# Last-tile bias by a one-row product, sums off GpSimd, and a new instruction order in a fused attention and dense kernel

## The chip, the cores and the metric

The kernel runs on one core of one Trainium2 chip. The metric is the device time of one launch in microseconds. Before the change the median of three runs is 163.94 us (163.46 to 164.64). The profiled execution took 163.67 us; the span of its trace, from the first instruction to the last, is 162.0 us.

A core has four engines that compute side by side: TensorE (PE, matrix products into PSUM), VectorE (DVE), ScalarE (ACT, activations) and GpSimd (POOL). SyncE (SP) starts most of the transfers (DMA). Each engine works through its own list of instructions in order, and engines wait for each other by semaphores. PSUM has 8 banks, each with 512 fp32 columns on 128 partitions.

## What is computed

The input is 2048 tokens of 448 bf16 values. After a layer norm, a windowed attention (16 heads, each token sees itself and seven earlier ones at a distance of two) and a two-layer dense branch with gelu run on the same normed tokens. The dense branch, through silu, gates the attention branch:

```python
def _B_ref(x, w1, b1, w2, b2):
    h = jnp.einsum("bsd,df->bsf", x, w1) + b1
    h = _gelu(h)
    return jnp.einsum("bsf,fd->bsd", h, w2) + b2

x = A_x
xn = _layernorm(x, axis=-1)
s = _A_ref(xn, A_wqkv, A_wo)      # attention, then its output product with wo
g = _silu(_B_ref(xn, B_w1, B_b1, B_w2, B_b2))
return x + s * g
```

silu(y) is computed as 0.5 * y * (tanh(y / 2) + 1), so that ScalarE needs only tanh. The inner width of the dense branch is 1792, that is 14 blocks of 128.

## The kernel before

Tokens are worked on in 16 tiles of 128 and in 4 chunks of 4 tiles. The kernel is not written in the order in which it runs. It is first written as a list of tasks with an engine, an estimated cost, dependencies, buffers and a priority; a planner goes through them in estimated time, and where several tasks could start on an engine it takes the one with the highest priority. The order that comes out is emitted, and is fixed on the chip. A task may name two engines; the planner then takes the one on which it ends first.

The first dense layer (FF1) of a chunk makes 14 blocks of h. Its contraction is 448 = 3 x 128 + 64, so each block takes three full products (`full`) and one on 64 rows (`tail`). Two tails on different halves of the array run side by side. A batch closes some blocks (full products, then the tail) and opens others (tail, then full products), so that its tails lie together:

```python
FF1 = (((3, 3), (2, 2), (2, 2)),      # per chunk: (closed, opened) of each batch
       ((3, 5), (3, 3)),
       ((2, 3), (2, 3), (2, 2)),
       ((4, 4), (2, 4)))
JOINED = (False, False, False, True)
```

```python
def batch(close, opened, prio):
    for j in close:
        ...  # three full products of j, taking a PSUM bank: L572 for FF1
    pairs = max(sum(j.half == h for j in every) for h in range(2))
    ...      # all tails of the batch, in pairs on the two halves: L575 for FF1
    for i, j in enumerate(opened):
        ...  # three full products of j
```

Each block leaves PSUM by a gelu on ScalarE (L579). Queries, keys and values are made in the same way (L513, L539 full; L516, L542 tails; `if JOINED[c] or not c` puts the values of a chunk into the batches of its queries and keys). The attention has products on 32 rows (QK, L651), an exp on ScalarE (L657), a mask on VectorE (L665) and the product with the values (L673).

The second dense layer of a tile, and what follows it up to the gate:

```python
def parts(t):
    n = D // 2 if t == NT - 1 else D          # the last tile goes in two halves of 224 columns
    return [(slice(c0, c0 + n), n, c0 + n == D) for c0 in range(0, D, n)]

def ff2_part(t, cs, n, end, prio):
    ...
        for mt in range(7 * i, 7 * i + 7):                               # L608, twice seven
            nc.tensor.matmul(ps[:, :n], h[...][:, j * P:(j + 1) * P], w2[:, mt, cs],
                             start=(mt == 0), stop=(mt == NMT - 1))
    ...
    def f2(k):                                                           # L624, y
        nc.vector.tensor_tensor(out=y[:, :n], in0=bank[:, :n], in1=b2[:, cs], op=ALU.add)
    def f3(k):                                                           # L630, tanh
        nc.scalar.activation(t[:, :n], y[:, :n], ACT.Tanh, scale=0.5)
    def f4(k):                                                           # L634, gate
        nc.vector.scalar_tensor_tensor(out=g[:, :n], in0=t[:, :n], scalar=1.0,
                                       in1=y[:, :n], op0=ALU.add, op1=ALU.mult)
```

(Buffer look-ups are shortened to the names of the tiles here.) The end of a tile starts when its attention is there and its dense part is done:

```python
def final_part(t, cs, n, g, prio):
    def f1(k):                                # L715: the output product, four matmuls
        ...
    a = plan.add("PE", pe(n, KT), f1, [t_oT[t]] + t_wo + [t_f2[t]], ...)
    def f2(k):                                # L720: sg = 0.5 * bank * g
        ...
    def f3(k):                                # L725: o = x + sg
        (nc.gpsimd if k.on == "POOL" else nc.vector).tensor_tensor(...)
    last = NT - 3 <= t < NT - 1
    o = plan.add(("DVE", "POOL") if last else "DVE", (dve(n, 2), 1.3) if last else dve(n, 2), f3, [s], ...)
    ...                                       # L732: the store, issued by SyncE
```

For tile 15 `t_f2` is the second half, so both of its output products come after all of its dense products. The gates of the last tiles lie in the buffer of `w_in`, which is free by then, and appear under that name in the trace.

Of the kernel before, what the change touches and what calls it, by code (L numbers as in the profile page):

```python
# [10 lines left out]
ALU = mybir.AluOpType  # L11
ACT = mybir.ActivationFunctionType
# [141 lines left out]
def kernel(  # L154
# [12 lines left out]
    nc = tc.nc  # L167
    P = 128
    S, D, H, DH, F = A_x.shape[1], 448, 16, 28, 1792
    assert tuple(A_x.shape) == (1, S, D) and S == 2048  # L170
    NT = S // P
# [4 lines left out]
    NMT = F // P  # L176
# [24 lines left out]
    def sb(name, shape, dt=BF16):  # L201
        return const.tile(shape, dt, name=name)
# [3 lines left out]
    x_sb = sb("x_sb", [P, NT, D])  # L206
# [8 lines left out]
    b2 = sb("b2", [P, D])  # L215
# [5 lines left out]
    ident = sb("ident", [P, P])  # L221
    eps_t = sb("eps_t", [P, 1], F32)
    half_t = sb("half_t", [P, 4], F32)
    m_gen = sb("m_gen", [P, 4, NQ])
    m_b0 = sb("m_b0", [P, 4, P])
    m_sp = sb("m_sp", [P, 4, NQ])
# [5 lines left out]
    def ring(name, n, shape, dt=BF16, fifo=False):  # L232
# [8 lines left out]
    p_y = ring("y", 2, [P, D], F32)  # L241
    p_t = ring("t", 2, [P, D], F32)
    p_g = ring("g", 4, [P, D])
    p_sg = ring("sg", 2, [P, D])
    p_o = ring("o", 3, [P, D])
# [6 lines left out]
    p_b = _Pool([psum.tile([P, 512], F32, name=f"bank{i}") for i in range(8)])  # L252
# [2 lines left out]


    FF1 = (((3, 3), (2, 2), (2, 2)),
           ((3, 5), (3, 3)),
           ((2, 3), (2, 3), (2, 2)),
           ((4, 4), (2, 4)))  # L260
    JOINED = (False, False, False, True)

    PRIO = {
                "project": (1, 122.5, 82, 27.5,),
                "project2": (164, 164.5, 166, 26.5,),
                "values": (186.5, 199, 146, 47,),
                "attn": (199, 199, 199, 167.5, 153.5, 147, 112.5, 99, 190, 169, 144, 105, 100, 84.5, 82,
            41.5, 31,),
                "ff1": (117, 79, 37, 125.5, 114.5, 15.5, 195, 187, 127.5, 198.5, 157, 4.5,),
                "gelu": (48, 103, 17, 103,),  # L270
                "ff2": (50, 55, 82, 88, 187.5, 82, 34, 14.5, 58.5, 5.5, 53.5, 9, 23.5, 102.5, 13.5, 1,),
                "final": (31.5, 36.5, 21.5, 191, 80.5, 62, 10.5, 20, 5.5, 67.5, 5.5, 1, 35.5, 37.5, 1, 1,),
                "norm": (173, 139.5, 108.5, 30, 30.5, 69.5, 156, 89.5, 71.5, 197, 51, 46, 85, 195, 51.5,
            70.5,),
                "stats": (59, 70, 70.5, 136.5, 65.5, 151.5, 60.5, 122.5, 172, 169, 93.5, 69, 64, 184.5,
            38.5, 57.5,),
                "turn_x": (92, 52, 134, 5, 66, 175, 52.5, 61.5, 30, 199, 125, 104.5, 32.5, 198, 196, 199,),
                "turn_qk": (89, 93, 5, 26, 185.5, 169, 35, 199, 51, 140, 126.5, 33.5, 18, 171, 118, 119.5,),
                "turn_o": (115, 170, 118, 26.5, 59, 153, 1, 8.5, 32, 37.5, 131, 1, 197, 192.5, 29.5,
            153.5,),  # L280
                "move_v": (52.5, 67.5, 27.5, 24.5, 1, 9.5, 90, 60, 161, 134.5, 168, 24, 192, 190.5, 1, 178,
            68.5,),
                "move_o": (106.5, 32, 154, 199, 148, 97, 97.5, 109.5, 57, 4.5, 76, 102.5, 178, 102.5, 28.5,
            103.5, 192.5,),
                "copies": (70, 169.5, 47.5, 44, 112, 161.5, 198.5, 181, 140.5, 16, 74, 140.5, 116, 199,
            81.5,),
    }
    LATER = {"qk": -30, "v": -27.5, "gelu": -30, "exp": 27.5, "mask": -29, "pv": -26, "recip": 9, "os": 26, "y": 60, "tanh": 49, "g": 49, "sg": 59, "o": 5.5}

    plan = _Plan()  # L290

    def buf(pool, owner, i=0):
        return pool.bufs[owner.slots[pool][i]]

    def pe(n, k=1):
        return k * (n / 2400.0 + 0.0025)

    def act(n):
        return 0.15 + n / 1130.0

    def dve(n, r=1):
        return 0.15 + n / (960.0 * r)
# [8 lines left out]
    def memset(eng, ap, v):  # L311
        def fn(_):
            getattr(nc, eng).memset(ap, v)
        return fn

    warm = p_h.bufs[-1]
    t_on = plan.add("DMA", 0.8, lambda _: None, (), 100)
# [15 lines left out]
    t_qz = [plan.add("DVE", 0.08, memset("vector", q[:, :, :, DH:], 0.0), [t_on], prio=95) for q in qk_tok]  # L333
    t_vw = [plan.add("DVE", 0.08, memset("vector", v[:, :, DH:], 1.0), [t_on], prio=96) for v in v_tok[:9]]
    t_os = [plan.add("POOL", 0.1, memset("gpsimd", o[:, D:], 0.0), [t_on], prio=94) for o in p_ot.bufs]
    t_wo = [plan.add("POOL", 0.45, memset("gpsimd", wo[64:, 3, :], 0.0), [t_on], prio=93)]
    t_E = [plan.add("POOL", 0.1, memset("gpsimd", e[:, :, NQ:], 0.0), [t_on], prio=95) for e in p_E.bufs]

# [225 lines left out]
    t_h = {}  # L564
# [22 lines left out]
    t_g = {}  # L587
    t_f2 = {}
    ff1_last = {}
# [10 lines left out]

    def ff2_part(t, cs, n, end, prio):
        c, j = divmod(t, TPC)
        halves = []
        for i in range(2):
            def f1(k, i=i):
                ps = buf(p_b, halves[0] if i else k)
                for mt in range(7 * i, 7 * i + 7):
                    nc.tensor.matmul(ps[:, :n], buf(*h_at[(c, mt)])[:, j * P:(j + 1) * P], w2[:, mt, cs],  # L608
                                     start=(mt == 0), stop=(mt == NMT - 1))
            if i:  # L610
                last = j == TPC - 1 and end
                halves.append(plan.add(
                    "PE", pe(n, 7), f1, [halves[0]] + [t_h[(c, mt)] for mt in range(7, NMT)] + t_w2[1]
                    + ([t_f2[q] for q in range(c * TPC, t)] if last else []),
                    prio + 0.5, give=tuple(h_at[(c, mt)] for mt in range(NMT)) if last else (),
                    tail=0.15))
            else:
                halves.append(plan.add("PE", pe(n, 7), f1, [t_h[(c, mt)] for mt in range(7)] + t_w2[0] + [ff1_last[c]],
                                       prio, take=(p_b,)))
        a = halves[1]  # L620
        t_f2[t] = a

        def f2(k):
            nc.vector.tensor_tensor(out=buf(p_y, k)[:, :n], in0=buf(p_b, halves[0])[:, :n], in1=b2[:, cs], op=ALU.add)  # L624
        if t == NT - 1:
            prio += 9
        y = plan.add("DVE", dve(n), f2, [a, t_b2], prio + LATER["y"], take=(p_y,), give=((p_b, halves[0], 0),))

        def f3(k):
            nc.scalar.activation(buf(p_t, k)[:, :n], buf(p_y, y)[:, :n], ACT.Tanh, scale=0.5)  # L630
        th = plan.add("ACT", act(n), f3, [y], prio + LATER["tanh"], take=(p_t,), table=("exp", "gelu"))

        def f4(k):
            nc.vector.scalar_tensor_tensor(out=buf(p_g, k)[:, :n], in0=buf(p_t, th)[:, :n], scalar=1.0,  # L634
                                           in1=buf(p_y, y)[:, :n], op0=ALU.add, op1=ALU.mult)
        t_g[t].append(plan.add("DVE", dve(n), f4, [th, y], prio + LATER["g"], take=(p_g,), give=((p_y, y, 0), (p_t, th, 0))))


    t_oT, ot_at = {}, {}
# [71 lines left out]
    def final_part(t, cs, n, g, prio):  # L711
        def f1(k):
            ps = buf(p_b, k)
            for kt in range(KT):
                nc.tensor.matmul(ps[:, :n], oT[:, kt, t * P:(t + 1) * P], wo[:, kt, cs],  # L715
                                 start=(kt == 0), stop=(kt == KT - 1))
        a = plan.add("PE", pe(n, KT), f1, [t_oT[t]] + t_wo + [t_f2[t]], prio, take=(p_b,), tail=0.15)

        def f2(k):
            nc.vector.scalar_tensor_tensor(out=buf(p_sg, k)[:, :n], in0=buf(p_b, a)[:, :n], scalar=0.5,  # L720
                                           in1=buf(p_g, g)[:, :n], op0=ALU.mult, op1=ALU.mult)
        s = plan.add("DVE", dve(n), f2, [a, g], prio + LATER["sg"], take=(p_sg,), give=((p_b, a, 0), (p_g, g, 0)))

        def f3(k):
            (nc.gpsimd if k.on == "POOL" else nc.vector).tensor_tensor(  # L725
                out=buf(p_o, k)[:, :n], in0=x_sb[:, t, cs], in1=buf(p_sg, s)[:, :n], op=ALU.add)
        last = NT - 3 <= t < NT - 1
        o = plan.add(("DVE", "POOL") if last else "DVE", (dve(n, 2), 1.3) if last else dve(n, 2), f3, [s], prio + LATER["o"],
                     take=(p_o,), give=((p_sg, s, 0),))

        def f4(_):
            nc.sync.dma_start(rows(o_half, t * P, P)[:, cs], buf(p_o, o)[:, :n])  # L732
        q = plan.add("SP", 0.55, f4, [o], 50)
        plan.add("DMA", 0.4, lambda _: None, [q], 50, give=((p_o, o, 0),), tail=1.2)
# [48 lines left out]
    def project(c):  # L783
# [19 lines left out]
        for b in blocks_of[c]:  # L803
# [11 lines left out]
    t_w2 = [[dma("POOL", w2[:, 7 * i:7 * i + 7, :], B_w2[F // 2 * i:F // 2 * (i + 1), :].rearrange("(m p) c -> p m c", p=P),  # L815
                 784, 84 - i, [t_hold])] for i in range(2)]
# [9 lines left out]
    for c, what in ((0, "F"), (1, "F"), (0, "A"), (1, "A"), (2, "F"), (2, "A"), (3, "A"), (3, "F")):  # L826
# [5 lines left out]
        else:  # L832
# [4 lines left out]
            i = 0  # L837
# [46 lines left out]
```

The softmax here doesn't subtract the row's maximum and nothing guards it: scores larger than these inputs give would overflow.

## Time and profile before

| | busy, us | share of the span | instructions |
|---|---|---|---|
| VectorE | 102.6 | 63% | 275 |
| ScalarE | 102.0 | 63% | 186 |
| GpSimd | 48.3 | 30% | 106 |
| DMA, 16 engines | | moved 20.80 MB, 128 GB/s | |

The granted TensorE clock is 0.987 of full speed. Line numbers such as L608 are those of the kernel before; in the changed kernel they move by some lines. The profile has a page (shares, the span in 40 slices, the chain of work that ended last, the costliest groups) and views on request, such as the instructions in order of time. In such a view a line gives the start in us, the duration in us, the engine, the line, the operation, what is written and read, the shapes, and at the end, in brackets, how long the engine sat idle before it and what released it. An "x7" means seven instructions merged into one line. In the chain, each piece is counted from the end of the one before it, so that its durations add up to the span, while durations of single matmuls overlap.

### The profile page before, as it was taken

The page shows a single profiled execution, that of the slowest core. Times are in us where ns is not written, and L with a number is a line of the kernel's source. Part 1 is how long each engine was busy: PE and PEld are TensorE (multiplying, and loading weights), DVE is VectorE, ACT ScalarE, POOL GpSimd, SP SyncE. Part 2 cuts the span into 40 slices and gives each one's busy share as a digit, 9 for nine tenths or more (in the row PEclk, how much of TensorE's full clock was granted, in tenths as well). Part 3 has the DMA queues.
Part 4 walks back from the last instruction along what each step waited for, and adds up shares of the span by engine and source line. Part 5 has one row for each costly group of instructions (what it writes and reads, how often), then busy time and mean ns, then how long its engine had stood idle before and what let it go on. Part 6 is the DMA issues. An engine that isn't in the chain of part 4 may idle for free.

```text
span 162.0 us, 3570 instructions
## 1 busy us (share of the span) xinstructions
PE 153.2 (95%) x1303; PEld 75.7 (47%) x1311; DVE 102.6 (63%) x275; ACT 102.0 (63%) x186; POOL 48.3 (30%) x106
## 2 busy tenths in 40 slices
PE   6999999999999999999999999999999999999940
PEld 2554333434444555445553334555555535455730
DVE  4978530395523988589892524897899994506760
ACT  3326597557587727788849577888798596722200
POOL 7306601971700050445735000037333300300020
PEclk9999999999999999999999999999999999999995
DMA  5999893799998252773968410067932450330110
GB/s 153 325 302 278 169 202 65 231 369 199 99 193 163 58 119 59 124 107 96 170 133 201 96 41 28 28 62 161 199 84 59 108 131 28 109 70 0 59 45 12
DMA packets 40733, 20.80 MB, mean 128 GB/s; under 512 B 34160, under 2 KB 38724, under 8 KB 40716
## 3 DMA queue, kind: packets, MB, share of 16 engines
q1 hardware_dynamic: 37372, 13.61, 44.0%
q0 software_dynamic: 3200, 6.85, 16.3%
q8 instruction: 10, 0.16, 0.5%
q10 hardware_dynamic: 144, 0.11, 0.3%
q14 instruction: 7, 0.06, 0.1%
HBM read 7.06 MB, written 1.84 MB: 55 GB/s over the span
## 4 chain that ended last, share of the span: by engine, by line
PE 90%; DVE 3%; issue 2%; DMA 2%; ACT 0%; DVEq 0%; ACTq 0%
PE bank L608 25%; PE bank L572 23%; PE bank L513 12%; PE bank L715 7%; PE bank L539 6%; PE bank L673 5%; PE bank L575 5%; PE bank L651 3%; PE bank L516 2%; DMA x_sb<-in_A_x_dram 2%; PE bank L542 1%; PE bank L443 1%; DVE st L397 1%; DVE y L624 1%; DVE sg L720 0%
## 5 line engine op out<-in xcount | busy, mean ns | idle before, releaser
L608 PE MATMUL bank<-w,h 128*128 128x448 bf16 (+1 forms) x238 | 46.6, 341 | 0.0
L579 ACT ACTIVATE h<-bank,b 128x512 bf16<-128x512 f32 x56 | 34.1, 696 | 9.9 <-PE bank L575 8.3
L572 PE MATMUL bank<-xnT,w 128*128 128x512 bf16 x160 | 38.0, 379 | 0.7 <-issue 0.5
L657 ACT ACTIVATE E<-bank 128x480 bf16<-128x480 f32 (+1 forms) x68 | 33.4, 580 | 6.6 <-PE bank L651 5.5
L348 POOL DMA_DIRECT2D ot<-os x31 | 16.7, 541 | 52.9 <-DVE os L685 50.1
L608 PEld LDWEIGHTS <-h 128*128 128x128 bf16 x238 | 21.9, 97 | 17.3 <-issue 0.2
L572 PEld LDWEIGHTS <-w 128*128 128x128 bf16 x168 | 15.7, 98 | 21.1 <-issue 3.8
L348 POOL DMA_DIRECT2D v<-v_tok x30 | 16.3, 548 | 29.8 <-PE bank L673 12.3
L665 DVE TENSOR_TENSOR E<-E,m_gen 128x480 bf16<-128x480 bf16 x60 | 21.4, 400 | 2.6 <-ACT E L657 2.3
L513 PE MATMUL bank<-w_in,xnT 128*128 128x448 bf16 x96 | 22.1, 352 | 0.0
L630 ACT ACTIVATE t<-y 128x448 f32<-128x448 f32 (+1 forms) x17 | 9.5, 559 | 16.0 <-DVE y L624 15.7
L624 DVE TENSOR_TENSOR y<-bank,b 128x448 f32<-128x448 f32 (+1 forms) x17 | 10.1, 594 | 7.5 <-PE bank L608 7.3
L715 PE MATMUL bank<-wo,oT 128*128 128x448 bf16 (+1 forms) x68 | 14.4, 341 | 0.0
L306 ACT CAST qk_tok<-bank 128x448 bf16<-128x448 f32 x22 | 11.3, 540 | 4.3 <-PE bank L513 2.2
L673 PEld LDWEIGHTS <-E 128*128 128x128 bf16 x272 | 10.6, 96 | 6.3 <-DVE g L634 0.7
L720 DVE SCALAR_TENSOR_TENSOR sg<-bank,g 128x448 bf16<-128x448 f32 x10 | 6.2, 620 | 9.9 <-ACT h L579 9.5
L539 PE MATMUL bank<-w_in,xnT 128*128 128x448 bf16 x48 | 11.9, 353 | 0.0
L513 PEld LDWEIGHTS <-xnT 128*128 128x128 bf16 x96 | 8.2, 97 | 7.3 <-issue 1.1
L431 DVE TENSOR_SCALAR xn<-x_sb,mv,rstd 128x448 bf16<-128x448 bf16 x16 | 6.4, 397 | 8.1 <-POOL rstd L418 4.5
L673 PE MATMUL bank<-v,E 128*128 128x29 bf16 x240 | 11.1, 176 | 0.0
L306 ACT CAST v_tok<-bank 128x448 bf16<-128x448 f32 x11 | 5.8, 536 | 8.3 <-PE bank L542 4.7
L685 DVE TENSOR_TENSOR os<-bank,rd 120x448 bf16<-120x448 f32 (+1 forms) x17 | 10.6, 624 | 0.6
(66 smaller groups left out, 135.5 us busy)
## 6 DMA issues: line engine op xcount, KB each, us to landing
out_dram<-o SPq DMA_DIRECT2D x15, 112.0 KB, 1.7
w<-in_B_w_dram POOLq DMA_DIRECT2D x2, 784.0 KB, 7.6
w<-in_B_w_dram SPq DMA_DIRECT2D x2, 672.0 KB, 6.9
w_in<-in_A_wqkv_dram SPq DMA_DIRECT2D x3, 336.0 KB, 4.4
x_sb<-in_A_x_dram POOLq DMA_DIRECT2D x2, 448.0 KB, 4.2
w<-in_B_w_dram SPq DMA_DIRECT2D x4, 112.0 KB, 6.8
x_sb<-in_A_x_dram SPq DMA_DIRECT2D x1, 448.0 KB, 6.4
wo<-in_A_wo_dram POOLq DMA_DIRECT2D x1, 336.0 KB, 9.3
```

Of the source, the lines that this page charges most:

```text
L306: nc.scalar.copy(o, i)
L348: nc.gpsimd.dma_start(dst(k), src())
L513: nc.tensor.matmul(ps[:, :D], xnT[:, kt, cs], w_in[:, kt, which * D:(which + 1) * D], start=start, stop=stop)
L539: nc.tensor.matmul(ps[:, :D], xnT[:, kt, k0:k0 + P], w_in[:, kt, 2 * D:], start=start, stop=stop)
L572: nc.tensor.matmul(ps[:], w1[:, kt, ms], xnT[:, kt, cs], start=start, stop=stop)
L579: nc.scalar.activation(buf(p_h, own, i)[:], buf(p_b, own, i)[:], ACT.Gelu_apprx_tanh, bias=b1[:, mt:mt + 1])
L608: nc.tensor.matmul(ps[:, :n], buf(*h_at[(c, mt)])[:, j * P:(j + 1) * P], w2[:, mt, cs], start=(mt == 0), stop=(mt == NMT - 1))
L624: nc.vector.tensor_tensor(out=buf(p_y, k)[:, :n], in0=buf(p_b, halves[0])[:, :n], in1=b2[:, cs], op=ALU.add)
L657: nc.scalar.activation(buf(p_E, k)[:, :, :nq], buf(p_b, a, hl)[:, :4 * nq].rearrange("p (g q) -> p g q", g=4), ACT.Exp, scale=SCALE)
L665: nc.vector.tensor_tensor(out=E[:, :, :nq], in0=E[:, :, :nq], in1=m[:, :, :nq], op=ALU.mult)
L673: nc.tensor.matmul(ps[:, h, :DH + 1], buf(p_E, e)[:, g, :], v[:, h, :DH + 1], start=True, stop=True)
L715: nc.tensor.matmul(ps[:, :n], oT[:, kt, t * P:(t + 1) * P], wo[:, kt, cs], start=(kt == 0), stop=(kt == KT - 1))
```

## The change

It takes the addition of b2 of the last tile from VectorE: a matrix `row0`, whose first row is ones and whose other rows are zeros, is multiplied with b2 as the first product of each half, so that PSUM holds the sum with the bias. Tanh and the gate of that tile then read PSUM and no y is made. The sums o of tiles 13 and 14 may no longer go to GpSimd. The batches of FF1 in chunk 1 are cut differently. And all priorities of the planner, with the offsets for single kinds of task (LATER), are replaced, so that the order on every engine is another one. It is for a shorter end of the kernel and for an order that suits it.

```diff
+    row0 = sb("row0", [P, P])
...
     FF1 = (((3, 3), (2, 2), (2, 2)),
-           ((3, 5), (3, 3)),
+           ((3, 3), (2, 2), (2, 2)),
            ((2, 3), (2, 3), (2, 2)),
            ((4, 4), (2, 4)))
-    JOINED = (False, False, False, True)
+    JOINED = (True, False, False, True)
     PRIO = {
...                                          (all 16 lists replaced; two shown)
-                "ff2": (50, 55, 82, 88, 187.5, 82, 34, 14.5, 58.5, 5.5, 53.5, 9, 23.5, 102.5, 13.5, 1,),
+                "ff2": (47, 66.5, 73, 94.5, 75, 143, 32, 5.5, 4.5, 48, 40, 2.5, 139.5, 83, 39, 26,),
-                "final": (31.5, 36.5, 21.5, 191, 80.5, 62, 10.5, 20, 5.5, 67.5, 5.5, 1, 35.5, 37.5, 1, 1,),
+                "final": (30.5, 42.5, 199, 138.5, 84, 5.5, 3, 2, 186.5, 2, 2, 1, 59.5, 167.5, 119, 168,),
...
-    LATER = {"qk": -30, "v": -27.5, "gelu": -30, "exp": 27.5, "mask": -29, "pv": -26, "recip": 9, "os": 26, "y": 60, "tanh": 49, "g": 49, "sg": 59, "o": 5.5}
+    LATER = {"qk": -15, "v": -30, "gelu": -29, "exp": -15, "mask": -30, "pv": -27, "recip": 35, "os": 27.5, "y": 59, "tanh": -11, "g": 6, "sg": 41, "o": 37.5}
...
+    t_row0 = plan.add("POOL", 0.1, memset("gpsimd", row0[:], 0.0), [t_on], prio=93)
+    t_row0 = plan.add("POOL", 0.1, memset("gpsimd", row0[:1, :], 1.0), [t_row0], prio=93)
...
+        biased = t == NT - 1
...
+                if biased and not i:
+                    nc.tensor.matmul(ps[:, :n], row0[:], b2[:, cs], start=True, stop=False)
...
-                                     start=(mt == 0), stop=(mt == NMT - 1))
+                                     start=(mt == 0 and not biased), stop=(mt == NMT - 1))
...
-        y = plan.add("DVE", dve(n), f2, [a, t_b2], prio + LATER["y"], take=(p_y,), give=((p_b, halves[0], 0),))
+        if biased:
+            y, pool, held = halves[0], p_b, ((p_b, halves[0], 0),)
+        else:
+            ...                                          (y as before, pool = p_y)
...
-            nc.scalar.activation(buf(p_t, k)[:, :n], buf(p_y, y)[:, :n], ACT.Tanh, scale=0.5)
+            nc.scalar.activation(buf(p_t, k)[:, :n], buf(pool, y)[:, :n], ACT.Tanh, scale=0.5)
...
-                                           in1=buf(p_y, y)[:, :n], op0=ALU.add, op1=ALU.mult)
+                                           in1=buf(pool, y)[:, :n], op0=ALU.add, op1=ALU.mult)
...
-            (nc.gpsimd if k.on == "POOL" else nc.vector).tensor_tensor(
-                out=buf(p_o, k)[:, :n], in0=x_sb[:, t, cs], in1=buf(p_sg, s)[:, :n], op=ALU.add)
-        last = NT - 3 <= t < NT - 1
-        o = plan.add(("DVE", "POOL") if last else "DVE", (dve(n, 2), 1.3) if last else dve(n, 2), f3, [s], prio + LATER["o"],
-                     take=(p_o,), give=((p_sg, s, 0),))
+            nc.vector.tensor_tensor(out=buf(p_o, k)[:, :n], in0=x_sb[:, t, cs], in1=buf(p_sg, s)[:, :n], op=ALU.add)
+        o = plan.add("DVE", dve(n, 2), f3, [s], prio + LATER["o"], take=(p_o,), give=((p_sg, s, 0),))
```

More of the change, by code (lines that the diff above doesn't have):

```diff
@@ L257 @@
     FF1 = (((3, 3), (2, 2), (2, 2)),
-           ((3, 5), (3, 3)),
+           ((3, 3), (2, 2), (2, 2)),
            ((2, 3), (2, 3), (2, 2)),
            ((4, 4), (2, 4)))
-    JOINED = (False, False, False, True)
+    JOINED = (True, False, False, True)
     PRIO = {
[L264 to L270, printed above, removed]
-                "ff2": (50, 55, 82, 88, 187.5, 82, 34, 14.5, 58.5, 5.5, 53.5, 9, 23.5, 102.5, 13.5, 1,),
-                "final": (31.5, 36.5, 21.5, 191, 80.5, 62, 10.5, 20, 5.5, 67.5, 5.5, 1, 35.5, 37.5, 1, 1,),
[L273 to L286, printed above, removed]
@@ new lines @@
+                "project": (176, 160.5, 62.5, 25.5,),
+                "project2": (196, 184.5, 152, 14.5,),
+                "values": (24.5, 194.5, 154.5, 6.5,),
+                "attn": (184, 184, 183, 166.5, 156.5, 152.5, 117.5, 114.5, 152, 149, 138, 68.5, 63.5, 61.5,
+            61.5, 37, 32.5,),
+                "ff1": (199, 160.5, 6, 191, 112, 192, 199, 195, 138.5, 97.5, 127, 1,),
+                "gelu": (97, 175.5, 197.5, 144.5,),
+                "ff2": (47, 66.5, 73, 94.5, 75, 143, 32, 5.5, 4.5, 48, 40, 2.5, 139.5, 83, 39, 26,),
+                "final": (30.5, 42.5, 199, 138.5, 84, 5.5, 3, 2, 186.5, 2, 2, 1, 59.5, 167.5, 119, 168,),
+                "norm": (190, 197, 198.5, 121, 177, 1, 61.5, 23, 173.5, 184.5, 40.5, 65, 117.5, 2, 11.5,
@@ new lines @@
+            83.5,),
+                "stats": (28.5, 1, 177.5, 2, 55, 118, 154.5, 183.5, 25, 33, 1.5, 45.5, 191, 111.5, 173,
+            189,),
+                "turn_x": (184, 199, 126, 1, 159, 41, 43, 6, 158, 62, 71, 1, 126.5, 185, 1, 22,),
+                "turn_qk": (106.5, 122.5, 23.5, 1, 37, 199, 69, 198.5, 97, 52.5, 91.5, 1, 94.5, 136, 199,
+            197,),
+                "turn_o": (147, 12.5, 16.5, 144.5, 112, 186, 16.5, 49.5, 188.5, 32.5, 184, 145, 191, 24,
+            165.5, 139,),
+                "move_v": (186, 65.5, 66, 1.5, 5, 9, 14.5, 1.5, 11.5, 77.5, 156, 4.5, 5, 6.5, 78, 5, 2,),
+                "move_o": (83.5, 71, 179.5, 199, 99.5, 124, 182, 191, 6.5, 113.5, 164, 112, 168, 132.5, 139,
@@ L287 @@
+            83.5, 124,),
+                "copies": (57, 47, 39, 147.5, 199, 127, 65.5, 190.5, 147, 126.5, 110.5, 163.5, 27, 147,
+            36,),
     }
-    LATER = {"qk": -30, "v": -27.5, "gelu": -30, "exp": 27.5, "mask": -29, "pv": -26, "recip": 9, "os": 26, "y": 60, "tanh": 49, "g": 49, "sg": 59, "o": 5.5}
+    LATER = {"qk": -15, "v": -30, "gelu": -29, "exp": -15, "mask": -30, "pv": -27, "recip": 35, "os": 27.5, "y": 59, "tanh": -11, "g": 6, "sg": 41, "o": 37.5}
     plan = _Plan()
@@ L617, in ff2_part @@
             else:
-                halves.append(plan.add("PE", pe(n, 7), f1, [t_h[(c, mt)] for mt in range(7)] + t_w2[0] + [ff1_last[c]],
+                halves.append(plan.add("PE", pe(n, 8 if biased else 7), f1,
+                                       [t_h[(c, mt)] for mt in range(7)] + t_w2[0] + [ff1_last[c]] + ([t_row0, t_b2] if biased else []),
                                        prio, take=(p_b,)))
@@ L621, in ff2_part, with f2 @@
         t_f2[t] = a
-        def f2(k):
-            nc.vector.tensor_tensor(out=buf(p_y, k)[:, :n], in0=buf(p_b, halves[0])[:, :n], in1=b2[:, cs], op=ALU.add)
         if t == NT - 1:
             prio += 9
-        y = plan.add("DVE", dve(n), f2, [a, t_b2], prio + LATER["y"], take=(p_y,), give=((p_b, halves[0], 0),))
+        if biased:
+            y, pool, held = halves[0], p_b, ((p_b, halves[0], 0),)
+        else:
+            def f2(k):
+                nc.vector.tensor_tensor(out=buf(p_y, k)[:, :n], in0=buf(p_b, halves[0])[:, :n], in1=b2[:, cs], op=ALU.add)
+            y, pool = plan.add("DVE", dve(n), f2, [a, t_b2], prio + LATER["y"], take=(p_y,), give=((p_b, halves[0], 0),)), p_y
+            held = ((p_y, y, 0),)
+        after = [a, y]
         def f3(k):
-            nc.scalar.activation(buf(p_t, k)[:, :n], buf(p_y, y)[:, :n], ACT.Tanh, scale=0.5)
-        th = plan.add("ACT", act(n), f3, [y], prio + LATER["tanh"], take=(p_t,), table=("exp", "gelu"))
+            nc.scalar.activation(buf(p_t, k)[:, :n], buf(pool, y)[:, :n], ACT.Tanh, scale=0.5)
+        th = plan.add("ACT", act(n), f3, after, prio + LATER["tanh"], take=(p_t,), table=("exp", "gelu"))
         def f4(k):
             nc.vector.scalar_tensor_tensor(out=buf(p_g, k)[:, :n], in0=buf(p_t, th)[:, :n], scalar=1.0,
-                                           in1=buf(p_y, y)[:, :n], op0=ALU.add, op1=ALU.mult)
-        t_g[t].append(plan.add("DVE", dve(n), f4, [th, y], prio + LATER["g"], take=(p_g,), give=((p_y, y, 0), (p_t, th, 0))))
+                                           in1=buf(pool, y)[:, :n], op0=ALU.add, op1=ALU.mult)
+        t_g[t].append(plan.add("DVE", dve(n), f4, [th] + after, prio + LATER["g"], take=(p_g,), give=held + ((p_t, th, 0),)))
     t_oT, ot_at = {}, {}
```

## Prediction, before the result was known

> **What bounds the kernel now.** I read the page's shares first, then the slices, then the chain that ended last, and then the order of instructions around its end.
>
> ```profile
> PE 153.2 (95%) x1303; PEld 75.7 (47%) x1311; DVE 102.6 (63%) x275; ACT 102.0 (63%) x186; POOL 48.3 (30%) x106
> PE   6999999999999999999999999999999999999940
> ...
> PE 90%; DVE 3%; issue 2%; DMA 2%; ACT 0%; DVEq 0%; ACTq 0%
> ```
>
> TensorE holds 90% of the chain and is full in 37 of 40 slices; the others have a third of the time free. But matmul records overlap, so "95% busy" does not show that it runs at its pace. I checked this from its own steps in the chain: seven matmuls of 448 columns take 1.32 us (189 ns each), four of 448 take 0.76, 29-column ones (P times V) 0.39 for sixteen. At that pace its work is: 210 x 0.189 + 28 x 0.096 for the second dense layer (42.4 us), 168 full matmuls and 28 pairs of half-height ones at 0.216 (512 columns, by the pace of the 448) for the first (42.3), 144 and 24 pairs at 0.189 for q, k, v (31.8), 60 x 0.189 + 8 x 0.096 for the output product (12.1), 6.7 for P times V, some 3.7 for QK (17 x 0.32 less the entry of 0.1) and 0.9 for transposes: about 140 us. It runs from 5.75 us to 155.5 us, 149.7 us. The 10 us between are mostly changes of tile shape, seen here in the chain in order of time:
>
> ```profile
> 42.05 1.94 PE bank L572 x9
> 43.99 0.75 PE bank L575 x6
> 44.75 1.43 PE bank L608 x7
> ...
> 48.12 1.32 PE bank L608 x7
> 49.44 0.41 PE bank L651 x16
> ```
>
> L575 and L651 are matmuls on 64 and 32 rows. Three pairs of L575 should take 3 x 0.216 = 0.65 and take 0.75; the seven of L608 behind them take 1.43, where the next seven take 1.32. So entering and leaving a tiled stretch cost about 0.1 us each. The chain has 10 stretches of L575, 10 of the halves of q, k, v and 17 of L651: 37 x 0.21 = 7.8 us. That leaves about 2 us of real waiting, half of it before 7 us. **The end** is different: here VectorE takes over.
>
> ```profile
> 153.18 0.39 ACT L630 ACTIVATE t<-y 128x224 f32<-128x224 f32 x1 [0.41 <-DVE y L624]
> 153.25 1.50 PE L608 MATMUL bank<-w,h 128*128 128x224 bf16 x14
> 153.72 0.62 DVE L720 SCALAR_TENSOR_TENSOR sg<-bank,w_in 128x448 bf16<-128x448 f32 x1
> 154.26 0.38 DVE L634 SCALAR_TENSOR_TENSOR w_in<-t,y 128x224 bf16<-128x224 f32 x1
> 154.43 1.10 POOL L725 TENSOR_TENSOR o<-x_sb,sg 128x448 bf16<-128x448 bf16 x1 [14.73 <-DVE sg L720]
> ...
> 154.59 0.93 PE L715 MATMUL bank<-wo,oT 128*128 128x224 bf16 x8
> 154.79 0.39 DVE L624 TENSOR_TENSOR y<-bank,b 128x224 f32<-128x224 f32 x1 [0.15 <-PE bank L608]
> 155.17 0.39 DVE L720 SCALAR_TENSOR_TENSOR sg<-bank,w_in 128x224 bf16<-128x224 f32 x1
> 155.27 0.39 ACT L630 ACTIVATE t<-y 128x224 f32<-128x224 f32 x1 [1.71 <-DVE y L624]
> 155.60 0.27 DVE L725 TENSOR_TENSOR o<-x_sb,sg 128x224 bf16<-128x224 bf16 x1
> 155.79 0.38 DVE L634 SCALAR_TENSOR_TENSOR w_in<-t,y 128x224 bf16<-128x224 f32 x1
> 156.31 0.39 DVE L720 SCALAR_TENSOR_TENSOR sg<-bank,w_in 128x224 bf16<-128x224 f32 x1
> 156.73 0.28 DVE L725 TENSOR_TENSOR o<-x_sb,sg 128x224 bf16<-128x224 bf16 x1
> ```
>
> The last product of the dense layer ends at 154.77 (the chain's reading). Six operations of VectorE follow with hardly a gap, in the order y, sg, o, gate, sg, o, up to 157.01: 2.24 us. The last store and the close of the program take the other 5.0 us of the span.
>
> **What the Trainium skill says.** "TensorE: Matmul & The Clock Gate", section Back-to-back issue gap, gives N/2.4 + 2.5 ns for matmuls in a row: 189 ns for 448 columns, 96 ns for 224. The trace agrees (1.32 us for seven). I take 0.096 us for each added product. "TensorEngine Tiling (Array Packing)", section Key Properties, says that a change of tiling mode drains the engine; the trace agrees and puts it at 0.1 us each way. "PSUM — Partial Sum Buffer", section Specifications (TRN2), lets ScalarE and VectorE read PSUM and GpSimd not; a VectorE instruction may take one tensor from it. The new gate takes the sum from PSUM and tanh from SBUF, so it needs no copy. "ScalarE: Activation LUTs", section What ACT_TABLE_LOAD costs, gives 186 + 0.833 N ns for an activation: 373 ns at 224 columns, an estimate; the trace has 390 from SBUF. No tanh here reads PSUM, but the exp on 480 columns from PSUM takes 579 ns and the tanh on 448 from SBUF 582, so I expect no more than 0.39.
>
> **The change part by part.**
>
> 1. *The bias on TensorE.* Tile 15 has two halves of 224 columns, each with one more product: 2 x 0.096 = **+0.19 us** on the engine that bounds.
>
> 2. *The two y of tile 15 go* (392 ns each). The first is off the path. The second starts the six operations of the end, so VectorE has 0.39 less to do. I count what it can start instead. Let E be the end of the last dense product. Tanh can start at E + 0.03 and is done at E + 0.42. The output product of the first half (four of 224 columns) is done at E + 0.40. Until then nothing at the end is ready: the gate needs that tanh, sg that product. Then come sg, o, gate, sg, o: 0.39 + 0.27 + 0.38 + 0.39 + 0.28 = 1.71, and 0.1 in gaps; E + 2.2. Before it was E + 2.24. So the sum's 0.39 us turn into a wait of 0.4 for tanh and product, and the gain is **-0.03 us**. In the most favourable order, with no gaps, it is -0.15.
>
> 3. *No sums on GpSimd.* The planner had the choice for tiles 13 and 14, and the trace shows one such sum, 1.10 us, ended at 155.53, long before the last o at 157.01. On VectorE it is a 0.39 us operation behind sg of tile 14, at about 154.3, and it can lie in the wait of step 2 and in the place of the first y: **0**. Its store goes out 0.8 us earlier, which nothing waits for.
>
> 4. *The first layer of chunk 1 in three batches*, (3,3), (2,2), (2,2), instead of (3,5), (3,3). Half-height pairs stay 4 + 3 = 3 + 2 + 2 = 7. There is one tiled stretch more: **+0.21 us**. On the other side, (3,5) needs eight banks of PSUM, all there are, and may make the product wait for evacuations; the chain shows one such wait of 0.16 us in that chunk. I count **-0.1**.
>
> 5. *All priorities are new.* This changes the order on every engine, and no amount of work. JOINED for chunk 0 has no effect, since chunk 0 is joined anyway. What a new order can win is the 2 us of waiting and tiled stretches that come to lie side by side (0.21 each). What it can lose is not limited so. All 16 lists and the offsets are replaced together, so they look fitted to the new plan, and I expect them to suit it better than the old ones would: **-0.5**, which is a choice and not a sum.
>
> 6. *Two memsets* on GpSimd at the start, of 0.2 us each (the ident's, as large, takes 205 ns), behind ident: 0, unless they push back the masks.
>
> Sum: 0.19 - 0.03 + 0 + 0.21 - 0.1 - 0.5 = -0.23, so 163.94 - 0.23 = 163.7 us.
>
> **The rivals.** *A: the last y was the path.* Then the end is shorter by 0.39 and a hop, and with a better order the time is 163.0. For it: y heads the chain's last six operations. Against it: the tanh of 0.39 us stands behind the same matmul and ended only 0.13 us before its gate got VectorE. *B: TensorE pays for all.* The added products and the stretch are 0.4 us, the new order gains nothing: 164.4. For it: TensorE is full and the old order left 2 us at most. Against it: the priorities were made anew for this very plan, which is only worth doing if the plan gets shorter. *C: the new order opens a wait* where transposes by DMA, GpSimd's moves or PSUM banks arrive late: one such wait of 1 to 3 us gives 165 to 167. For it: GpSimd's issues sit behind VectorE and TensorE by up to 18 us in the list of waits. Against it: most of those waits have slack, and a wait of TensorE is filled by the other branch. *D: the order wins much*, half of the 2 us and four merged stretches: 162.1. I hold it for rare.
>
> **Range and chances.** All that is stated by the change's words is within 0.4 us either way. The spread comes from the order: I take about 0.9 us either way. The three runs of before lie between 163.46 and 164.64, which adds some 0.3. So 8 times in 10 the time is within 162.5 and 165.2; the upper side is the longer one because a bad wait has no bound. Two per cent is 3.3 us: more than the whole waiting of TensorE, so faster by that 3%, slower by that 4%, within 93%.
>
> **What would show it.** Step 1: 30 products of 224 columns at L608's successor instead of 28. Step 2: no y of 224 columns, and VectorE idle for about 0.4 us ahead of the last five operations, released by tanh or the output product; if instead the time from the last dense product to the last o falls below 1.9 us, rival A was right. Step 3: no sum on GpSimd. Step 4: 11 stretches of L575's successor. Step 5: the time between TensorE's first transpose and last product, 149.7 before; with 0.4 us of added work, above 150.1 means that the order gained nothing, and a gap of TensorE released by a DMA or an evacuation is rival C. My number is wrong if this time moves by over 1.3 us.

## The result, and the profile after

The changed kernel takes 162.01 us (median of four runs, 161.90 to 162.34). Beside it the kernel before took 164.16. The ratio is 0.988, with a 95% interval of 0.984 to 0.992. The time fell by 2.1 us, where 0.2 was predicted, and lies below the predicted range.

On the page of the changed kernel almost nothing moves:

```profile
PE 154.1 (96%) x1305; PEld 75.4 (47%) x1313; DVE 102.6 (64%) x274; ACT 101.8 (64%) x186; POOL 47.5 (30%) x107
PE   6999999999999999999999999999999999999990
...
PE 94%; DVE 2%; issue 2%; ACT 0%; ACTq 0%; DVEq 0%
```

TensorE is as full as it was, and its busy time is even 0.9 us longer. The mean granted clock is 0.987 before and 0.995 after, but between 8 and 150 us it is 1.00 in both, so it is not the cause. So the end has to be read. These are the last instructions of the changed kernel in order of time (start, duration, engine, line, what is written and read, idle time before and its releaser); the dense product is now L615, the output product L728, gate, sg and o are L647, L733 and L738:

```profile
153.90 1.50 PE L615 MATMUL bank<-w,h 128*128 128x224 bf16 x14
154.53 0.39 DVE L738 TENSOR_TENSOR o<-x_sb,sg 128x448 bf16<-128x448 bf16 x1
154.83 0.38 DVE L647 SCALAR_TENSOR_TENSOR w_in<-t,bank 128x224 bf16<-128x224 f32 x1
155.24 0.93 PE L728 MATMUL bank<-wo,oT 128*128 128x224 bf16 x8
155.44 0.36 ACT L643 ACTIVATE t<-bank 128x224 f32<-128x224 f32 x1 [1.02 <-PE bank L615]
155.82 0.39 DVE L733 SCALAR_TENSOR_TENSOR sg<-bank,w_in 128x224 bf16<-128x224 f32 x1 [0.61 <-PE bank L728]
156.25 0.28 DVE L738 TENSOR_TENSOR o<-x_sb,sg 128x224 bf16<-128x224 bf16 x1
156.44 0.38 DVE L647 SCALAR_TENSOR_TENSOR w_in<-t,bank 128x224 bf16<-128x224 f32 x1
156.93 0.39 DVE L733 SCALAR_TENSOR_TENSOR sg<-bank,w_in 128x224 bf16<-128x224 f32 x1
157.35 0.28 DVE L738 TENSOR_TENSOR o<-x_sb,sg 128x224 bf16<-128x224 bf16 x1
```

The last o ends at 157.63. In the kernel before it ended at 157.01. **The work ends 0.6 us later than before, and the span is 1.8 us shorter** (160.2 instead of 162.0). So the gain lies wholly behind the last o: the close took 4.99 us before and takes 2.57 now. A store explains less than half of the 4.99; in the table of transfers (count, size of one, median us from issue to landing) the kernel before has:

```profile
out_dram<-o SPq DMA_DIRECT2D x15, 112.0 KB, 1.7
```

Neither the busy times nor the chain show what fills the rest, because they leave out the sequencers' own instructions. A view of the program's last line has them. Each line gives an engine's queue, the operation, how many, shortest, median and longest in ns, and the first and last start. The kernel before:

```profile
L879 POOLq EVENT_SEMAPHORE  x4: 17/17/17, 161.2 to 161.9; - x4
L879 POOLq DRAIN  x3: 46/106/6789, 154.4 to 161.7; - x3
L879 SPq DRAIN  x3: 7/7/13, 158.8 to 161.4; - x3
```

The changed kernel:

```profile
L889 POOLq EVENT_SEMAPHORE  x4: 17/17/17, 159.5 to 160.1; - x4
L889 POOLq DRAIN  x3: 46/106/6204, 139.3 to 159.9; - x3
L889 SPq DRAIN  x3: 7/7/13, 159.4 to 159.7; - x3
```

GpSimd closes with a DRAIN of over 6 us. It begins as soon as GpSimd's last instruction has been handed out, and only behind it comes GpSimd's first closing semaphore. Before, it began at 154.4, with the sum o of tile 14, and ended at 154.4 + 6.79 = 161.2; that sum ended at 155.53, so the drain lasted 5.66 us behind it. The program ends 0.8 us after that. SyncE had been done with the last store since 158.8 and waited. In the changed kernel GpSimd's last instruction is a transfer issued at 139.3, and its drain is over at 145.5, while TensorE still has over 10 us of work. The end then follows the last store.

The waits of SyncE show the same thing under another name. Before and after, with the total, the count and the longest:

```profile
SPq L879 <- PEq L879: 3.0, 2, 2.5
```

```profile
SPq L889 <- PEq L889: 0.7, 2, 0.5
```

The releaser named is TensorE's sequencer. TensorE had been done for more than five microseconds (its last product ended at 155.5). The wait is at the common barrier, and it ends with whoever arrives last, which was GpSimd.

**Theory D** follows from this: the end is the later of GpSimd's last instruction plus 5.7 + 0.8 us and the last o plus 2.6 us, and the whole gain is that one sum on GpSimd is gone. The rivals are **O**, the new order and the shorter chain of the last tile, and **S**, a close that was long because the last stores came close together.

### The profile page after: what moved, and what is told of

Read it like the earlier page. It is cut to its first block, busy times and chain, and to the rows that moved or that the text cites. A ratio compares the mean times of both kernels' runs of the same rounds, so it can differ in the third digit from the quotient of the medians.

```text
span 160.2 us, 3579 instructions
## 1 busy us (share of the span) xinstructions
PE 154.1 (96%) x1305; PEld 75.4 (47%) x1313; DVE 102.6 (64%) x274; ACT 101.8 (64%) x186; POOL 47.5 (30%) x107
## 4 chain that ended last, share of the span: by engine, by line
PE 94%; DVE 2%; issue 2%; ACT 0%; ACTq 0%; DVEq 0%
PE bank L615 25%; PE bank L575 23%; PE bank L516 12%; PE bank L728 7%; PE bank L542 6%; PE bank L686 5%; PE bank L578 5%; PE bank L664 3%; PE bank L322 3%; PE bank L519 2%; PE bank L545 1%; PE bank L446 1%; DVE sg L733 1%; DVE y L637 0%; ACT E L670 0%
## 5 line engine op out<-in xcount | busy, mean ns | idle before, releaser
L615 PE MATMUL bank<-w,h 128*128 128x448 bf16 (+1 forms) x238 | 46.7, 341 | 0.0
L575 PE MATMUL bank<-xnT,w 128*128 128x512 bf16 x160 | 38.7, 380 | 0.5 <-issue 0.2
L615 PEld LDWEIGHTS <-h 128*128 128x128 bf16 x238 | 21.9, 97 | 17.3 <-issue 0.4
L643 ACT ACTIVATE t<-y 128x448 f32<-128x448 f32 x15 | 8.8, 585 | 13.0 <-DVE y L637 12.9
L728 PE MATMUL bank<-wo,oT 128*128 128x448 bf16 (+1 forms) x68 | 14.1, 341 | 0.0
L637 DVE TENSOR_TENSOR y<-bank,b 128x448 f32<-128x448 f32 x15 | 9.3, 622 | 6.6 <-PE bank L615 6.2
L400 DVE BATCH_NORM_STATS2 st<-x_sb 128x6 f32<-128x448 bf16 x16 | 9.7, 608 | 4.2 <-DMA x_sb<-in_A_x_dram 4.2
L733 DVE SCALAR_TENSOR_TENSOR sg<-bank,g 128x448 bf16<-128x448 f32 x10 | 6.1, 618 | 9.5 <-ACT h L582 9.5
```

Of the source, the lines that this page charges most:

```text
L575: nc.tensor.matmul(ps[:], w1[:, kt, ms], xnT[:, kt, cs], start=start, stop=stop)
```

## The experiments

**Only the sum moved.** The kernel before, with o always on VectorE. The order on TensorE is the same in the two traces, instruction by instruction; only this one sum has another place.

```diff
-        o = plan.add(("DVE", "POOL") if last else "DVE", (dve(n, 2), 1.3) if last else dve(n, 2), f3, [s], ...)
+        o = plan.add("DVE", dve(n, 2), f3, [s], ...)
```

> The kernel before, with the one sum on GpSimd (tile 14's o) moved to VectorE; nothing else changes its place. Theory D (the end is set by GpSimd's closing drain, which lasts 5.7 us behind its last instruction): GpSimd is done near 140 us, the last o ends at about 157.2 and the close takes 2.6 us behind it, as in the changed kernel. Span 159.8 to 160.1, time 161.5 to 161.8, the whole gain. Theory O (the new order and the shorter chain of the last tile made the gain): nothing changes, 163.7 to 164.2. Theory S (the close was long because the last three stores came close together): the store of tile 14 goes out earlier, so some of the gain, 162.5 to 163.5.

Measured: 162.01 us (161.61 to 162.61), ratio to the kernel before 0.989 (0.986 to 0.992), against 163.92 for the kernel before on the same chip. This one instruction brings 1.9 us, the changed kernel's time within 0.01 us. The profiled run was the slowest of the four, 162.61, with a span of 160.9, above the 160.1 that I had written. Its trace says why: TensorE waited once near the start for a block of the weights w_in, which it did not in the trace of the kernel before.

```profile
8.60 0.54 PE L513 MATMUL bank<-w_in,xnT 128*128 128x448 bf16 x2 [0.98 <-DMA w_in<-in_A_wqkv_dram]
```

From this product on (7.59 us in the kernel before) both traces take 147.2 us to the last dense product. Without the wait the span would be near 159.9 by this estimate, as expected; the median is 0.2 above its expected range. The last o ends at 158.04, and the close behind it is 2.9 us rather than 2.6, because the last two o end together and SyncE issues their stores one behind the other, the second 0.27 us after its o. O is wrong as the main cause.

**Only the product.** The old order, the bias by the product, and the sum of tile 14 named to be on GpSimd (with the product in it the planner itself would no longer choose GpSimd).

```diff
+        biased = t == NT - 1        # row0 times b2 ahead of the last tile's products, no y
-        o = plan.add(("DVE", "POOL") if last else "DVE", ...)
+        o = plan.add("POOL" if t == NT - 2 else "DVE", ...)
```

> The kernel before, with its old order and its sum of tile 14 on GpSimd, but with the last tile's bias by the product with the one-row matrix. D: the sum on GpSimd still ends near 155.5 and its drain near 161.2; span about 162, time 163.6 to 164.2, no gain. O, if the product is the gain: 162 to 163.

Measured: 163.80 us, ratio 1.001 (0.998 to 1.003). The trace has its last two o together, the later one ending at 156.76, earlier than in any other kernel with GpSimd at the end. It brings nothing: behind it the drain runs to 154.1 + 6.71, near 160.9. (The chain ends on the first of the two, at 156.57; a later expectation takes that for the last o.)

```profile
156.31 0.45 DVE L738 TENSOR_TENSOR o<-x_sb,sg 128x224 bf16<-128x224 bf16 x2
...
L891 POOLq EVENT_SEMAPHORE  x4: 17/17/17, 160.9 to 161.5; - x4
L891 POOLq DRAIN  x3: 46/106/6714, 154.1 to 161.4; - x3
```

**The sum put back into the changed kernel.** All orders stay as in the changed kernel.

```diff
-        o = plan.add("DVE", dve(n, 2), f3, [s], ...)
+        o = plan.add("POOL" if t == NT - 2 else "DVE", 1.3 if t == NT - 2 else dve(n, 2), f3, [s], ...)
```

> The changed kernel with the sum of tile 14 put back on GpSimd. Sg of that tile ends at 154.5, so the sum ends near 155.7. D: drain until 161.4, span about 162.2, time 163.7 to 164.1: the whole gain is lost. O: the order and the product are still there, so 161.9 to 162.3.

Measured: 163.77 us, ratio 0.999 (0.997 to 1.001). The whole gain is gone. Its last o ended at 157.28, the drain at 154.2 + 6.72 = 160.9, and the span was 161.7:

```profile
L891 POOLq DRAIN  x3: 46/102/6716, 154.2 to 161.4; - x3
```

**A small instruction at the end of GpSimd.** The changed kernel plus one copy of 8 elements on one partition. This parts D from S, since no store is touched.

```diff
+    mark = sb("mark", [P, 8])
+        if t == NT - 1 and n + cs.start == D:
+            plan.add("POOL", 0.12, lambda _: nc.gpsimd.tensor_copy(mark[:1, :], buf(p_o, o)[:1, :8]), [o], 1)
```

> The changed kernel with one more instruction on GpSimd, a copy of 1x8 elements out of the last o into a tile that nobody reads. It costs about 0.2 us and holds up no store. D: it ends near 158.0, the drain near 163.7, span 164.5, time 166.0 to 166.4, 4 us more than the changed kernel. O and S: 162.0 to 162.3.

Measured: 165.78 us (165.36 to 166.25), ratio 1.012 (1.009 to 1.015): 3.8 us more than the changed kernel, a little less than expected. The copy and GpSimd's closing, in two views:

```profile
157.75 0.18 POOL L742 COPY mark<-o 1x8 bf16<-1x8 bf16 x1 [17.80 <-DVE o L739]
```

```profile
L892 POOLq DRAIN  x3: 46/102/5847, 157.7 to 164.1; - x3
```

157.7 + 5.85 = 163.6, and the span is 164.4. SyncE was done with the stores at 159.4. An instruction of 0.18 us costs twenty times its duration. The close is long without any change to a store, so S is wrong as the cause; stores that come close together are worth the 0.3 us seen above.

**The same copy a little earlier**, out of the o of tile 13.

```diff
-        if t == NT - 1 and n + cs.start == D:
+        if t == NT - 3:
```

> The changed kernel with the same small GpSimd copy, but out of the o of tile 13, which ends at 151.8 in the changed kernel. D: the copy ends near 152.1, the drain near 157.8, before the last store has landed at about 159.2; so it costs nothing, 161.9 to 162.3. If any late instruction of GpSimd costs time in itself, and not by its drain: 163 or more.

Measured: 161.81 us (161.32 to 162.45), ratio 0.988 (0.984 to 0.992), no difference to the changed kernel. Its drain is just as long, but ends before the stores have landed:

```profile
L892 POOLq DRAIN  x3: 46/106/5847, 151.7 to 159.8; - x3
L892 SPq DRAIN  x3: 7/7/13, 159.3 to 159.6; - x3
```

151.7 + 5.85 = 157.6, and SyncE is done at 159.3. So the instruction itself is free and its drain costs only what stands out behind the last store.

**What the drain is made of.** Three kernels that leave out all of the reference: x is loaded, VectorE works for 29 us on it, 16 tiles are stored, and GpSimd makes one small copy at the end. They differ in what GpSimd issues before.

```diff
+    for i in range(30):                                     # second kernel: none
+        nc.gpsimd.dma_start(z_sb[:, i % 4, :], x_sb[:, i % NT, :])
+    for i in range(45):                                     # third kernel, instead
+        nc.gpsimd.dma_start(z_sb[:8, i % 4, :], x_sb[:8, i % NT, :])
     ...
+    nc.gpsimd.tensor_copy(mark[:1, :], o[NT - 1][:1, :8])
```

> A kernel of its own that leaves out all of the reference: x is loaded, VectorE doubles it (six times over, for time), 16 stores; GpSimd issues 30 transfers from SBUF to SBUF early and one copy of 1x8 at the end. D: the closing drain lasts 5.6 to 5.8 us behind the copy, as in the full kernel.

> The same without any transfer issued by GpSimd. If the drain is a fixed cost of GpSimd's close: again 5.6 to 5.8 us behind the copy. If it is what cleans up behind transfers that GpSimd issued: under 1 us.

> The small kernel of its own again (all of the reference left out), with 45 transfers issued by GpSimd instead of 30, each of 8 rows instead of 128, and the same copy of 1x8 at the end. The 30 transfers left a drain of 2.56 us behind the copy, 0.085 us each, and 68 of all sizes in the full kernel 5.66, 0.083 each. If the drain goes by the number of transfers: 3.8 us behind the copy. If it goes by rows or bytes: 0.3 us or little more.

Measured, one execution each, with 30 large transfers, with none, and with 45 small ones:

```profile
L70 POOLq DRAIN  x3: 34/101/2739, 37.3 to 40.6; - x3
```

```profile
L70 POOLq DRAIN  x3: 34/76/266, 37.6 to 40.0; - x3
```

```profile
L70 POOLq DRAIN  x3: 34/101/3961, 37.8 to 42.3; - x3
```

Each includes the copy of 0.18 us. The first expectation failed: the drain is no fixed 5.7 us. Without transfers it is 0.09 us behind the copy, with 30 it is 2.56, with 45 small ones 3.78. Over the empty one that is 0.082 us for each transfer, at 128 rows (112 KB) and at 8 rows (7 KB) alike. The 17 transfers of SyncE, which all three have, add nothing that shows. The full kernel issues 68 transfers from GpSimd (7 loads, and 30 and 31 moves of v and of the attention's result): 68 x 0.082 + 0.09 = 5.67, and 5.66 was read. A full kernel with fewer transfers on GpSimd was not tried.

**The rest of the change.** Since the sum alone brings the whole gain, what do the product and the new order do? Two kernels without any late GpSimd work answer this: the old order with the product, and the new order with y.

```diff
     FF1, PRIO, LATER                                        # old_dve_prod: those of before
+        biased = t == NT - 1
-        o = plan.add(("DVE", "POOL") if last else "DVE", ...)
+        o = plan.add("DVE", ...)
```

> The kernel before with both parts named in the change's words, and the old order and batches: no sum on GpSimd, bias of the last tile by the product. Theory N (without the drain, the product gives back what it takes): as the kernel with the sum on VectorE alone, 161.7 to 162.3. Theory G (y was on the path, as rival A of the prediction had it): 0.4 less, 161.3 to 161.6; the trace of the old order with product and GpSimd sum, whose last o ended at 156.6, speaks for it. Theory O2 (the new order loses time against the old one): about 161.5, below the changed kernel by 0.4, which is what one more tiled stretch and the new order cost on TensorE.

```diff
-        biased = t == NT - 1                                # new_y: the changed kernel, without row0
+        biased = False
```

> The changed kernel with y of the last tile put back on VectorE, and without the one-row product and its matrix. N: TensorE is done 0.19 earlier, VectorE has one more operation of 0.39 at the end; 161.8 to 162.1, no difference. G: 162.3 to 162.6, 0.4 more than the changed kernel.

| order | bias | o of tile 14 | time, us | ratio to before, 95% interval |
|---|---|---|---|---|
| old | y | GpSimd | 163.92 (before) | 1 |
| old | product | GpSimd | 163.80 | 1.001 (0.998 to 1.003) |
| new | product | GpSimd | 163.77 | 0.999 (0.997 to 1.001) |
| old | y | VectorE | 162.01 | 0.989 (0.986 to 0.992) |
| old | product | VectorE | 161.56 | 0.986 (0.983 to 0.989) |
| new | y | VectorE | 162.42 | 0.992 (0.988 to 0.995) |
| new | product | VectorE | 162.01 (changed kernel) | 0.988 (0.984 to 0.992) |

Each ratio is to the kernel before measured beside it, which took 163.86 to 164.16. With the sum on GpSimd nothing else counts. Without it, the medians give the product 0.45 us in the old order and 0.41 in the new, and the new order a cost of 0.41 to 0.45. But the intervals overlap, so this is not settled, and the traces agree with it only in part. First the old order, the last dense product and the last two o, with y and with the product:

```profile
154.43 1.36 PE bank L608 x14
...
157.59 0.45 DVE L725 TENSOR_TENSOR o<-x_sb,sg 128x224 bf16<-128x224 bf16 x2
```

```profile
153.40 1.34 PE bank L615 x14
...
156.26 0.45 DVE L738 TENSOR_TENSOR o<-x_sb,sg 128x224 bf16<-128x224 bf16 x2
```

That is 2.25 us from one to the other with y and 1.97 with the product. Of the 0.28, 0.19 goes to the two added products, so 0.1 us is won here and not 0.45. In the new order it is more, because with y VectorE reaches the end late. Here is a part of the chain of the new order with y, in order of time:

```profile
153.99 1.35 PE bank L613 x14
155.34 0.62 DVE sg L731
...
155.99 0.39 DVE o L736
156.38 0.31 DVE y L635
```

The chain leaves TensorE before its last product and goes over sg and o of tile 14 to the first y, which had waited for them. From the last dense product (156.68) to the last o (159.51) it takes 2.83 us, where the changed kernel takes 2.23. The 0.60 less 0.19 for the two added products is 0.41.

The cost of the new order is not in the work that it gives TensorE. From TensorE's fourth product with w_in, where that wait for weights lay, to its last dense product the traces show 147.4 us in the old order with the product (sum on either engine) and 147.4 in three kernels of the new order with the product, although the new order has one tiled stretch more. Three other traces of the new order take longer, all of it before 37 us: the changed kernel 0.2 us, the kernel with the early output product below 0.6, the one with y 1.2. The view of waits names transposed xn in the last two (0.3 us each) and a gelu in the last (0.5); that one was profiled in its slowest run, 163.80. No trace of the old order shows this. It would be rival C of the prediction on a small scale, but with so few traces it is not shown.

**A better end.** The output product of the first half of tile 15 is put ahead of the dense products of the second half, so that sg and o of the first half are done before.

```diff
-    a = plan.add("PE", pe(n, KT), f1, [t_oT[t]] + t_wo + [t_f2[t]], ...)
+    own = t_half[-2] if t == NT - 1 and not cs.start else t_f2[t]     # its own half's dense product
+    a = plan.add("PE", pe(n, KT), f1, [t_oT[t]] + t_wo + [own], ...)
```

> The changed kernel, with the output product of the first half of tile 15 put ahead of the dense products of the second half. Only TensorE's order changes. The last dense product ends 0.40 later, at 155.8, but sg and o of the first half are then done before it; behind it stand tanh 0.36, gate 0.38, sg 0.39, o 0.28 and hops of 0.15 in all, so the last o ends at 157.35 instead of 157.63. With theory D the end now follows the last o: 0.28 less, 161.7. If VectorE is behind at that point, no change, 162.0.

> The old order with the sum on VectorE, the product, and the output product of the first half early. N: 0.2 to 0.3 below the changed kernel, 161.7 to 161.8. G or O2: 161.0 to 161.4, the fastest of all.

Measured: 161.85 us with the new order, ratio 0.987 (0.984 to 0.990), and 161.29 with the old one, ratio 0.985 (0.982 to 0.988). In the trace of the first, VectorE is no longer behind; the chain is one instruction of each kind:

```profile
154.67 1.35 PE bank L616 x14
...
156.05 0.36 ACT t L645
...
156.44 0.40 DVE w_in L649
...
156.93 0.40 DVE sg L737
...
157.36 0.27 DVE o L742
```

From the last dense product to the last o it is 156.01 to 157.63, 1.62 us, where the changed kernel takes 2.23; the four products put ahead take 0.38, so 0.23 is won, where 0.28 was expected. In the times it is 0.16, within the spread. In the old order the same step takes this interval from 1.97 to 1.62, which the four products use up; there the close falls from 2.9 to 2.6 us, since the last two o no longer end together. The last kernel has the lowest median of all, 2.6 us below the kernel before, but its interval overlaps that of the old order with the product (161.56) and that of the changed kernel; that it is the fastest is not shown.

## Why the prediction was wrong

- **What bounds the kernel** was right up to the last o and wrong behind it. The prediction wrote "The last store and the close of the program take the other 5.0 us of the span" and took them for fixed. The table of transfers says 1.7 us from issue to landing, so 3.3 us of those 5.0 were unexplained, in plain sight.
- **Step 1**, the bias on TensorE, was right: two products of 224 columns, and the chain counts 0.10 us for each. The Trainium skill, "TensorE: Matmul & The Clock Gate", section Back-to-back issue gap, gives the formula used there for a matmul on its own, and for a stream another pace, about 131 ns at 512 columns; here fourteen products of 224 columns in a row take 1.35 us, 96 ns each, as the formula has it, and the measurement decides.
- **Step 2**, the y of tile 15, was right in its mechanism and its number. From the last dense product to the last o the prediction had 2.2 us, and the trace has 155.40 to 157.63, 2.23, with an idle time of 0.61 ended by the output product. Its order of the last five operations is the one in the trace. In the new order, with all sums on VectorE, the old y would have cost more (2.83); in the old order it would not (2.25). So the place of the sum alone does not make the product worth more.
- **Step 3**, no sums on GpSimd, **is the step that failed**: it put the gain at 0, since the sum "ended at 155.53, long before the last o at 157.01" and its store was one "which nothing waits for". The sum and its store had slack. The engine's drain behind it had not: 155.53 + 5.66 + 0.8 = 162.0 is the span. Moving the sum alone measured 1.9 us.
- **Step 4**, one more tiled stretch, is as predicted: the list of waits has 11 entries into L578, the tails of FF1, where the kernel before had 10. What this alone costs was not tried; together with the new order it adds nothing to TensorE's 147.4 us.
- **Step 5**, the new order, was put at -0.5 by choice. TensorE from its first transpose to its last product took 150.3 us (5.87 to 156.17), against 149.8, and the prediction had said that above 150.1 the order gained nothing. But this time has the wait for w_in in it, and two traces with the same order on TensorE, the kernel before and the one with only the sum moved, have 149.8 and 150.9; behind it the two orders are equal, so the -0.5 is not there. The medians put the order at 0.41 to 0.45 us lost, the stretch of step 4 included, with overlapping intervals.
- **Step 6** was right: the memsets push GpSimd's masks back by 0.4 us and nothing of that reaches TensorE.
- **The rivals.** B was right that the order gains nothing. A, about y, was wrong for the kernel before and holds only in the new order, once the sums are on VectorE. D named 162.1, next to the 162.01 measured, but by a gain of the order that did not come: a hit by luck. None of the four saw the close. All looked for the end of the last work, and none asked which engine arrives last at the barrier. The sign set for a wrong number, a move of TensorE's time by over 1.3 us, could not show it either: that time moved by 0.5.

The sum with the medians' terms, from the kernel before: -1.9 for the drain, -0.4 for the product, +0.4 for order and batches, that is -1.9; 2.1 was measured, and the spread of either kernel is larger than the difference. Of these terms only the first is shown.

## What to carry to other kernels

Subtract the end of the last useful instruction and the landing of its store from the span. The changed kernel has 0.9 us left, the kernel before had 3.3; where clearly more than the former is left, list the closing instructions of every engine's queue and see who is last. On GpSimd, help at the very end is paid for with its whole close, and that close grows with every transfer that it has issued in the program. So GpSimd has to do its last work early; that another engine should issue its transfers would follow too, but was not tried in the full kernel. While such a close governs, no saving on the chain that the profile shows brings anything, as the product in the old order showed.

## What the runs showed of the hardware

GpSimd's closing DRAIN is not constant: 0.09 us behind its last instruction without transfers of its own, 2.56 after 30, 3.78 after 45, 5.66 after 68, about 0.082 us for each transfer, large or small. The last of these transfers had been issued 4.5 to 15 us before, and the small kernels' took 1.6 to 2.1 us to land (median). The Trainium skill, "VectorE: DVE Perf Modes", section The DRAIN you can't avoid, says of the DRAINs at the start and end of a program that they take a constant 12 ns or so on all five engines. That fits SyncE here (7 to 13 ns) and not GpSimd (up to 6.8 us with the last instruction in it), nor the first closing ones of TensorE, ScalarE and VectorE (1.9, 0.4 and 0.3 us in the kernel before); the measurement decides. What the drain does for each transfer the runs don't show. Tanh of 224 columns took 0.36 us from PSUM where it had taken 0.39 from SBUF, and the gate took 0.38 from either.
